# Strassen's seven products for two of three column groups of a bilinear feed-forward layer, with single buffers for turned attention weights

## The chip, the cores and the metric

The kernel runs on one core of a Trainium2 chip. The metric is the device time of one execution in microseconds (us). The kernel before takes 1522.86 us, the median of three runs (1520.39 to 1523.19).

## The reference

Thresholded attention feeds a bilinear feed-forward network, all in fp32. What is computed, cut to what matters:

```python
batch, n_heads, seq, head_dim = (8, 8, 576, 64)
scores = scale * np.matmul(q, k.transpose(0, 1, 3, 2))
thresh = np.max(scores, axis=-1, keepdims=True) - tau
scores = np.where(scores >= thresh, scores, -1000000000.0)
attn = np.exp(scores - np.max(scores, axis=-1, keepdims=True))
attn = attn / (np.sum(attn, axis=-1, keepdims=True) + 1e-09)
x = np.matmul(attn, v)            # heads put side by side: 4608 tokens x 512
a = x @ w_a                       # 512 x 1536
b = x @ w_b                       # 512 x 1536
out = a * b @ w_out               # 1536 x 512
```

The weights come as 8-byte floats and are turned to fp32 on the chip.

## The kernel before, in words

**Attention.** The work is cut into 32 pairs of heads (8 batches x 4 pairs, `HP` = 4). Each pair has five units `u`: four of 128 queries (u = 0 to 3), for both heads, and one of the 64 queries that are left over, with both heads in one. That makes 160 units `g`. The list `units` orders them by batch: first u = 0 and 1 of each of four pairs, then u = 2, 3 and 4 of each. The first batch has an order of its own. A unit runs like this:

- `scores` (L308): TensorE (PE) multiplies q and k into one PSUM tile per head (L318, a score tile `sc`). VectorE (DVE) takes the row maximum (L325), GpSimd (POOL) makes of it the exponent's bias and the threshold (L326, L327).
- `weigh` (L330): ScalarE (ACT) takes the exponent (L338), DVE zeroes what is under the threshold and sums (L342). After L342 the score tile's PSUM is free. `normalise` (L358) scales by the reciprocal.
- `turn_blocks` (L399), one unit later: DVE transposes the weights by 32 x 32 blocks into a tile `tb` (L407). u = 0 or 2 opens a new `tb`, u = 1 or 3 fills it and issues four DMAs on SyncE's (SP's) queue that write it to a scratch tensor `swap` in DRAM (L417). Unit 4 goes by a tile of its own (L422, L429).
- `turn_back` (L434), called at the head of the next unit: one DMA reads `swap` back as the turned weights `wT` (L440).
- `weighted` (L497), four units after the scores (`PV_LAG`): PE multiplies v and `wT` (L455, in `product`), ACT and DVE join the halves into a block `x` of 256 tokens (L444, L445).

The first eight units turn their weights by PE (`turn_pe`, L371).

**The feed-forward network.** 4608 tokens make 18 blocks of 256 tokens: two per batch and two of the left-over queries. `exchange_blocks` (L467) has POOL copy the two 64-row halves of a finished `x` crosswise into `xS` (L465), since all matmuls are on 64 x 64 tiles, four at a time, and each half of the rows must meet each half of the weights. `ffn` (L519) is a generator: it yields after each step of four matmuls and tells how many columns went through. The first layer has three groups of 512 hidden columns; each is two pieces `f` for two weights (`wa_sb`, `wb_sb`), and each of these is an accumulation of eight steps of 256 columns into one PSUM tile `pab` (L544). ACT copies the first into `h` (L550), DVE multiplies the second into it (L552). The second layer (L564, PSUM tile `po`) runs two accumulations of twelve steps of 512 columns, which ACT and DVE join into `osb`, and SP stores (`store`, L581). The very first block has four pieces at 128 columns, so that it can begin when half its tokens are there.

**What sets the order.** `keep_order` (L37) fixes each engine's order to that in which the program was written. In the loop over `g` (L644) every unit writes its attention work and, in four portions between them, a number of feed-forward columns by `advance` (L589): at most 0.09 of a block's, plus what replaces the weighted sums, and less when the backlog would run out before the next block is there. `make_room` (L610) places the weighted sums well inside an accumulation. PSUM is one pool, `banks` (L124), of four tiles of two banks each, which go round in turn: score tiles, `pab`, `po`, `pv` and transposes all take the next one.

**Buffers.** SBUF tiles are given out by tag: 7 for `xT` (x, xS, the left-over `xt`, raw weights), 2 each for `tb` and `wT`, 3 for loaded q and k, 4 for attention weights `w`, 6 for `h`, 5 for `osb`. A new tile of a tag waits until the readers of the one whose place it takes are done. The conversion of weights (`load_weights` to `convert_add`, L186 to L239) runs in the first 18 units, two or three pieces a unit.

Of the kernel before, what the change touches and what calls it, by code (L numbers as in the profile page):

```python
# [24 lines left out]
XT_BUFS = 7  # L25
W_BUFS = 4
WT_BUFS = 2
# [6 lines left out]
PORTIONS = (0.3, 0.35, 0.15, 0.2)  # L34

# [15 lines left out]
def kernel(  # L51
# [10 lines left out]
):  # L62

# [69 lines left out]
    def load(i, name, engine=nc.sync):  # L133

        b, hp = pairs[i]
        src = {"q": q, "k": k}[name]
        t = loads.tile([P, NB, Q], FP32, tag="qk", bufs=3, name=name + "m")
        for j in range(2):
            rows = src[b, 2 * hp + j].rearrange("(n e) d -> e n d", e=Q)
            for h in range(2):  # L140
                r = slice((2 * j + h) * Q, (2 * j + h + 1) * Q)
                engine.dma_start(t[r], rows[:, :, h * Q:(h + 1) * Q])  # L142
        loaded.setdefault(i, {})[name] = t
# [39 lines left out]
    raws, stages, extra = {}, {}, []  # L183
    state = {"loaded": 0, "converted": 0, "rows": 0}

    def load_weights(limit, engine=nc.sync):  # L186

        while (len(raws) < limit or extra) and state["loaded"] < NPIECES:
            n = state["loaded"]
            if len(raws) < limit:  # L190
                raw = work.tile([P, CW, 2], U32, tag="xT", bufs=XT_BUFS, name="raw")
            else:
                raw = extra.pop(0)
            src = pieces[n][1]
            for r, part in enumerate(src):
                dst = raw.rearrange("p f w -> p (f w)")[r * D:r * D + P // len(src)]
                if len(src) == 2:
                    dst = dst.rearrange("p (k f) -> p k f", k=2)
                engine.dma_start(dst, part)
            raws[n] = raw  # L200
            state["loaded"] = n + 1
# [46 lines left out]
    rooms = []  # L248
    for _ in range(2):
        t = work.tile([P, 2 * NB, 2 * Q], FP32, tag="tb", bufs=2, name="rows")  # L250
        t = t.rearrange("p n e -> p (n e)")[0:R]
        rooms += [t[:, c:c + 2 * NR * D].rearrange("p (n w) -> p n w", n=NR)
                  for c in range(0, 6 * NR * D, 2 * NR * D)]
    load_rows(0, "q", rooms[0])
    load_rows(0, "k", rooms[1], nc.scalar)
    load_rows(1, "q", rooms[2])
    load_rows(1, "k", rooms[3], nc.scalar)
    nc.sync.dma_start(tau_sb, tau.to_broadcast([P, 1]))
    load_weights(2)
    load_rows(2, "q", rooms[4])  # L260
    load_rows(2, "k", rooms[5])
    load_weights(4)
    load_v(0)
    for name in ("q", "k"):
        t = work.tile([P, CW, 2], FP32, tag="xT", bufs=XT_BUFS, name="rows")
        t = t.rearrange("p n e -> p (n e)")[0:R, 0:2 * NR * D]
        load_rows(3, name, t.rearrange("p (n w) -> p n w", n=NR))
# [103 lines left out]
    def turn_pe(i, u):  # L371

        ws, dg = weights.pop((i, u))
        wT = work.tile([P, NSLOT, P], FP32, tag="wT", bufs=WT_BUFS, name="wT")
# [24 lines left out]
    def turn_blocks(i, u):  # L399

        ws, _ = weights.pop((i, u))
        if u < NT:
            if u % 2 == 0:
                tbufs[i] = work.tile([P, 2 * NB, 2 * Q], FP32, tag="tb", bufs=2, name="tb")
# [11 lines left out]
            for g in range(G):  # L416
                nc.sync.dma_start(  # L417
                    swap[:, :, g * 2 * Q:(g + 1) * 2 * Q].rearrange("c p w -> p c w"),
                    tb[g * Q:(g + 1) * Q])
        else:  # L420
# [5 lines left out]
            for g in range(G):  # L426
                c = slice((1 - g // 2) * NB, (2 - g // 2) * NB)
                w0 = swap.shape[2] - TAIL + (g % 2) * Q
                nc.sync.dma_start(swap[c, :, w0:w0 + Q].rearrange("c p w -> p c w"),  # L429
                                  tb[g * Q:(g + 1) * Q])  # L430
        if part(i, u):
            ready.append(part(i, u))

    def turn_back():  # L434

        while ready:
            i, h = ready.pop(0)
            n = width(i, h)
            wT = work.tile([P, NSLOT, n], FP32, tag="wT", bufs=WT_BUFS, name="wT")
# [19 lines left out]
    def x_tile(name):  # L459
        return work.tile([P, HP, HALF], FP32, tag="xT", bufs=XT_BUFS, name=name)  # L460

# [4 lines left out]

    def exchange_blocks():  # L467
        while complete:
            x, what = complete.pop(0)
            xs = x_tile("xS")  # L470
            for hp in range(HP):
                exchange(x, xs, hp, 0, HALF, nc.gpsimd)
            blocks.append(((x, xs), what))
# [3 lines left out]
    def exchange_dma():  # L477
        while exchanges:
# [3 lines left out]
            if hp == HP - 1:  # L482
                state["rows"] = c1 // P
                if c0 == 0:
                    blocks.append(((x, xs), ("first", 0, 0)))

    def weighted_unit(i, u):
# [3 lines left out]
        if (b, 0) not in x_of:  # L491
            x_of[b, 0] = x_tile("xT")
            state["xs"] = x_tile("xS")
        join(x_of[b, 0][:, hp, u * P:(u + 1) * P], pv[:, 0], pv[:, 1])
        exchanges.append((x_of[b, 0], state["xs"], hp, u * P, (u + 1) * P))

    def weighted(i, h):  # L497
# [11 lines left out]
        if n % HALF:  # L509
            t = b % GT  # L510
            if hp == 0 and t == 0:
                xtail_of[b // GT] = x_tile("xt")
            join(xtail_of[b // GT][:, hp, t * TAIL:(t + 1) * TAIL], pv[:, 0, n - TAIL:n], pv[:, 1, n - TAIL:n])
            del loaded[i], prepared[i]
            if hp == HP - 1 and t == GT - 1:
                complete.append((xtail_of.pop(b // GT), ("tail", b - t, 0)))


    def ffn(xT, what):  # L519
# [3 lines left out]
        x, xs = xT  # L523
        hs = []
        n = CH // P
        steps = [(f, 0, HALF) for f in range(NG * n)]
        if kind == "first":
            steps = [(f, c, c + P) for c in (0, P) for f in range(2 * n)] + steps[2 * n:]
        for f, c0, c1 in steps:
            while (state["converted"] < 2 * HP * (f // n + 1)  # L530
                   or kind == "first" and state["rows"] * P < c1):
                yield 0, 0
            fs = f % n * P
            if c0 == 0:
                hs.append(work.tile([P, 2, HALF], FP32, tag="h", bufs=H_BUFS, name="h"))
            ht = hs[f][:, :, c0:c1]
            for w in (wa_sb, wb_sb):
                pab = banks(c1 - c0, "pab")
                for k in range(H):
# [7 lines left out]
                    if k < H - 1:  # L547
                        yield c1 - c0, (H - 1 - k) * (c1 - c0)
# [4 lines left out]
                yield c1 - c0, 0  # L553
        for u in range(2):
            po = banks(DM, "po")
            for F in range(NF):
                while state["converted"] < NPIECES - NF + F + 1:
                    yield 0, 0
                ht = hs[F // (2 * n) * n + F % n][:, F // n % 2]
                for r in range(2):  # L560
                    rows = slice(r * D, (r + 1) * D)
                    for c in range(2):
                        t0 = u * P + c * D
                        nc.tensor.matmul(po[c * D:(c + 1) * D, r], ht[rows, t0:t0 + D], wo_sb[rows, F, :],  # L564
                                         start=(F == 0), stop=(F == NF - 1))
                if F < NF - 1:
                    yield DM, (NF - 1 - F) * DM
# [9 lines left out]
            yield DM, 0  # L577
# [9 lines left out]
    running = {"ffn": None, "owed": 0.0, "left": 0, "done": 0, "rest": 0}  # L587

    def advance(cols):  # L589
        running["owed"] += cols  # L590
        while running["owed"] > 0:
            if running["ffn"] is None:
                if not blocks:
                    running["owed"] = 0.0
                    return
                running["ffn"] = ffn(*blocks.pop(0))
                running["left"] = BLOCK_COLS
            step, rest = next(running["ffn"], (None, 0))
# [5 lines left out]
            else:  # L604
# [3 lines left out]
                running["rest"] = rest  # L608

    def make_room():  # L610

        while running["rest"] and not (running["done"] >= ROOM and running["rest"] >= ROOM):
# [5 lines left out]
    def backlog():  # L618
        return len(blocks) * BLOCK_COLS + (running["left"] if running["ffn"] is not None else 0)
# [24 lines left out]
    for g in range(len(units) + PV_LAG):  # L644
# [6 lines left out]
        turn_back()  # L651
# [16 lines left out]
        if g == 3:  # L668
            for _ in range(2):
                t = work.tile([P, 2 * NB, 2 * Q], U32, tag="tb", bufs=2, name="raws")  # L670
                t = t.rearrange("p n e -> p (n e)")
                extra += [t[:, c:c + 2 * CW].rearrange("p (f w) -> p f w", w=2) for c in (0, 2 * CW)]
        load_weights(5 if g < 10 else 4)
        if g > BY_PE and g <= len(units):
            turn_blocks(*units[g - 1])
# [12 lines left out]
        if g > BY_PE:  # L688
            advance(PORTIONS[1] * pace)
            n = g - PV_LAG  # L690
            if BY_PE <= n < len(units) and part(*units[n]):
                make_room()
                weighted(*part(*units[n]))
                running["owed"] -= (NSLOT + 1) // 2 * width(*part(*units[n]))
        for n in early.get(g, [])[:1]:
# [12 lines left out]
        load_weights(5 if g < 10 else 4)  # L708
# [10 lines left out]
    exchange_blocks()  # L719
    while blocks or running["ffn"] is not None:  # L720
# [35 lines left out]
```

## Time and profile before

| what | value |
|---|---|
| median of three runs | 1522.86 us (1520.39 to 1523.19) |
| the profiled execution, its own time | 1518.81 us |
| its span, from the first to the last instruction | 1516.9 us |
| mean granted TensorE clock | 0.994 |
| scores L318, PE busy | 249.8 us |
| first layer L544, PE busy, all rows | 1048.8 us |
| second layer L564, PE busy | 423.2 us |
| weighted sums L455, PE busy | 190.0 us |
| HBM read and written | 127.40 and 89.65 MB |

Busy times of groups overlap, since matmuls are pipelined: the PE rows add to more than the span. PE stands for TensorE's matmuls and PEld for its weight loads. Each fp32 matmul leaves two records of each kind, so a step of four matmuls shows as eight. A row of the profile gives the line, the engine and the operation, then what it writes and reads, the shape and the count; after the first bar the busy time in us and the mean duration in ns, after the second the idle time of the engine just before and what ended it. A row of a timeline gives the start and the duration in us, and merged instructions show as a count.

### The profile page before, as it was taken

How to read it: one execution, taken by the hardware profiler on the slowest of the kernel's cores; microseconds unless marked ns; L12 is line 12 of the kernel's file. 1: busy time of each engine (PE TensorE's matmuls, PEld its weight loads, DVE VectorE, ACT ScalarE, POOL GpSimd, SP SyncE). 2: the span in 40 equal slices, each digit the busy share in tenths (PEclk: the TensorE clock that was granted, in tenths of full speed). 3: DMA queues.
4: the chain of work that ended last, by engine and by line, in shares of the span. 5: the costliest groups of instructions: out<-in, count | busy, mean ns of one | idle time of the engine just before them, and what ended most of it. 6: DMA issues, size and time to landing. Idle time of an engine off the chain costs nothing.

```text
span 1516.9 us, 51632 instructions
## 1 busy us (share of the span) xinstructions
PE 1461.7 (96%) x22896; PEld 1139.6 (75%) x22896; DVE 848.3 (56%) x1838; ACT 587.8 (39%) x929; POOL 262.3 (17%) x662
## 2 busy tenths in 40 slices
PE   6777999999999999999999999999999999999998
PEld 4666586786978587778877887777877978687775
DVE  5667676667656765675545755576646665510000
ACT  4766344444443443443333433343433443410000
POOL 2766211111110111020100101011111111110000
PEclk9999999999999999999999999999999999999999
DMA  9858888788868976796547966588748876530000
GB/s 204 177 149 217 174 164 192 179 160 192 193 148 159 192 182 150 145 195 144 123 106 146 195 145 145 124 173 176 183 90 162 184 180 132 123 75 16 2 16 15
DMA packets 625839, 220.93 MB, mean 146 GB/s; under 512 B 543184, under 2 KB 613328, under 8 KB 625616
## 3 DMA queue, kind: packets, MB, share of 16 engines
q1 hardware_dynamic: 623248, 217.04, 65.2%
q8 instruction: 180, 2.95, 0.8%
q10 hardware_dynamic: 2368, 0.59, 0.2%
q14 instruction: 43, 0.35, 0.1%
HBM read 127.40 MB, written 89.65 MB: 143 GB/s over the span
## 4 chain that ended last, share of the span: by engine, by line
PE 85%; DVE 4%; SPq 4%; DMA 3%; ACT 2%; issue 1%; POOL 0%; DVEq 0%; ACTq 0%; POOLq 0%
PE pab L544 45%; PE po L564 22%; PE sc L318 9%; PE pv L455 9%; SPq L417 2%; SPq L142 1%; DVE mx L325 1%; SPq L429 1%; DVE tb L407 1%; PE tp L380 1%; DVE low L231 0%; DVE w L342 0%; DMA swap<-tbt 0%; DMA wT<-swap 0%; DMA xS<-xT 0%
## 5 line engine op out<-in xcount | busy, mean ns | idle before, releaser
L564 PE MATMUL po<-wo_sb,h 64*64 64x512 f32 x3456 | 423.2, 589 | 0.0
L325 DVE TENSOR_REDUCE mx<-sc 128x1 f32<-128x576 f32 x288 | 205.1, 749 | 220.2 <-PE sc L318 213.8
L564 PEld LDWEIGHTS po<-wo_sb,h 64*64 64x64 f32 x3456 | 225.4, 133 | 130.5 <-issue 72.8
L338 ACT ACTIVATE w<-sc,bias,scalars 128x576 f32<-128x576 f32 x288 | 226.9, 827 | 186.7 <-POOL bias L326 181.4
L544 PE MATMUL pab<-xS,wa_sb 64*64 64x256 f32 (+1 forms) x3584 | 277.7, 370 | 4.4 <-POOL xS L465 3.3
L544 PE MATMUL pab<-xS,wb_sb 64*64 64x256 f32 (+1 forms) x3584 | 277.1, 371 | 0.5 <-issue 0.5
L361 ACT ACTIVATE w<-w,rcp 128x576 f32<-128x576 f32 x272 | 197.7, 768 | 182.0 <-DVE rcp L355 182.0
L326 POOL TENSOR_SCALAR bias<-mx,scalars 128x1 f32<-128x1 f32 x288 | 90.3, 316 | 1022.3 <-DVE mx L325 616.8
L318 PE MATMUL sc<-kT,qT 64*64 64x288 f32 x2304 | 249.8, 413 | 16.2 <-DVE kT L306 7.5
L544 PE MATMUL pab<-xT,wb_sb 64*64 64x256 f32 (+1 forms) x3200 | 248.3, 369 | 5.5 <-DVE h L552 3.9
L544 PE MATMUL pab<-xT,wa_sb 64*64 64x256 f32 (+1 forms) x3200 | 245.7, 370 | 4.1 <-POOL thr L327 2.1
L342 DVE SCALAR_TENSOR_TENSOR w<-sc,thr,w 128x576 f32<-128x576 f32 x288 | 222.4, 804 | 18.5 <-ACT w L338 15.8
L544 PEld LDWEIGHTS pab<-xS,wa_sb 64*64 64x64 f32 x3584 | 193.7, 133 | 36.8 <-POOL xS L465 10.1
L544 PEld LDWEIGHTS pab<-xS,wb_sb 64*64 64x64 f32 x3584 | 196.3, 134 | 28.2 <-issue 2.0
L544 PEld LDWEIGHTS pab<-xT,wa_sb 64*64 64x64 f32 x3200 | 174.6, 134 | 30.7 <-issue 3.3
L544 PEld LDWEIGHTS pab<-xT,wb_sb 64*64 64x64 f32 x3200 | 175.7, 133 | 27.9 <-DVE h L552 4.4
L455 PE MATMUL pv<-wT,vm 64*64 64x320 f32 (+3 forms) x2592 | 190.0, 381 | 5.6 <-ACT h L550 2.8
L318 PEld LDWEIGHTS sc<-kT,qT 64*64 64x64 f32 x2304 | 146.6, 135 | 56.6 <-issue 14.1
L407 DVE STREAM_TRANSPOSE tb<-w 128x576 f32<-128x576 f32 x240 | 171.4, 752 | 1.3 <-ACT w L361 1.3
L455 PEld LDWEIGHTS pv<-wT,vm 64*64 64x64 f32 x2592 | 146.3, 135 | 32.7 <-issue 7.7
L552 DVE TENSOR_TENSOR h<-h,pab 128x512 f32<-128x512 f32 (+1 forms) x112 | 73.1, 653 | 132.8 <-PE pab L544 128.9
L550 ACT COPY h<-pab 128x512 f32<-128x512 f32 (+1 forms) x112 | 63.5, 567 | 200.1 <-PE pab L544 199.6
(62 smaller groups left out, 702.8 us busy)
## 6 DMA issues: line engine op xcount, KB each, us to landing
swap<-tb SPq DMA_DIRECT2D x240, 288.0 KB, 5.3
wT<-swap SPq DMA_DIRECT2D x28, 1440.0 KB, 7.3
wT<-swap SPq DMA_DIRECT2D x32, 1152.0 KB, 6.2
vm<-in_v_dram SPq DMA_DIRECT2D x32, 288.0 KB, 4.8
swap<-tbt SPq DMA_DIRECT2D x128, 72.0 KB, 2.8
out_dram<-osb SPq DMA_DIRECT2D x32, 256.0 KB, 5.0
qm<-in_q_dram SPq DMA_DIRECT2D x112, 72.0 KB, 3.5
km<-in_k_dram SPq DMA_DIRECT2D x112, 72.0 KB, 4.6
```

The lines of the kernel that those rows point to most:

```text
L318: nc.tensor.matmul(sc[j if u < NT else 0][to, c], qT[r, q0:q0 + D], kT[r, c * SH:(c + 1) * SH], start=True, stop=True)
L325: nc.vector.tensor_reduce(mx[:, c], sc[j], axis=AX.XY, op=ALU.max)
L326: nc.gpsimd.tensor_scalar(bias[:, c], mx[:, c], e_nscale, None, op0=ALU.mult)
L338: nc.scalar.activation(w.rearrange("p (c k) -> p c k", c=2), s, AF.Exp, bias=bias[:, j:j + 1], scale=e_scale)
L342: nc.vector.scalar_tensor_tensor(out=wv, in0=s, scalar=thr[:, j:j + 1], in1=wv, op0=ALU.is_ge, op1=ALU.mult, accum_out=sums[:, j:j + 1])
L361: nc.scalar.activation(w, w, AF.Copy, scale=rcp[:, j:j + 1])
L407: nc.vector.transpose(tb[:, j * NB:(j + 1) * NB, (u % 2) * Q:(u % 2 + 1) * Q], w.rearrange("p (n e) -> p n e", e=Q))
L455: nc.tensor.matmul(pv[j * D:(j + 1) * D, r], vm[rows, k0], wT[rows, k0], start=(s == (NT if j == r else 0)), stop=(s == NT - 1))
L544: nc.tensor.matmul(pab[c * D:(c + 1) * D, r], w[rows, f // n, k, fs + c * D:fs + (c + 1) * D], moving, start=(k == 0), stop=(k == H - 1))
L550: nc.scalar.copy(ht, pab)
L552: nc.vector.tensor_tensor(ht, ht, pab, op=ALU.mult)
L564: nc.tensor.matmul(po[c * D:(c + 1) * D, r], ht[rows, t0:t0 + D], wo_sb[rows, F, :], start=(F == 0), stop=(F == NF - 1))
```

## The change

The first layer's products `x @ w_a` and `x @ w_b` of two of the three column groups (`STRASSEN` = 2) are done in the form of Strassen and Winograd. For such a group, tokens, inner dimension and hidden columns are each halved, which makes quarters X11 to X22 and W11 to W22. Eight products of quarters become seven of sums of quarters. One such product for both weights is eight steps of 128 columns, into a PSUM tile `seven`; it is emptied by ACT (two of seven) or by a DVE addition (five of seven) into tiles `kept` (tag `osb`); POOL makes two more sums and the four products a x b of the quarters.

- `weight_sums` makes three sums per group and weight, once, on POOL, and later replaces the quarter W12 by W11 - W12 in place. `token_sums` makes four sums per block, T1 to T4, on POOL, and their crosswise copies `tS`. Blocks whose exchange is written before the weights' sums are ready have no sums and go the old way; in the program as built this is the first block alone.
- In a block with sums, the direct group runs first, then the two groups by seven products, and the second layer takes the groups in that order.
- `exchange_blocks` takes a new block only when the block before has left its first layer.
- Room: `wT` and `tb` have one buffer instead of two, loaded q and k two instead of three. x tiles have three, xS, t and tS share three, `xt` has one. Raw weights and the first rows of q and k lie in the room of the sums until these are made.
- `turn_back` issues at most one read-back: only when no turned weights are waiting, and not in the unit that wrote the swap; it is called at the head of a unit and again after `weighted`.
- `advance`, `make_room` and `backlog` count a block's columns by its kind; room is at most half of an accumulation.

The diff, cut to its core:

```diff
-XT_BUFS = 7
-WT_BUFS = 2
+X_BUFS = 3
+STRASSEN = 2
...
-        t = loads.tile([P, NB, Q], FP32, tag="qk", bufs=3, name=name + "m")
+        t = loads.tile([P, NB, Q], FP32, tag="qk", bufs=2, name=name + "m")
...
+    NSUM = STRASSEN * 2 * 3 * HP * P
+    sums_u32 = const.tile([P, NSUM], U32, name="sums_u32")
...
-                tbufs[i] = work.tile([P, 2 * NB, 2 * Q], FP32, tag="tb", bufs=2, name="tb")
+                tbufs[i] = work.tile([P, 2 * NB, 2 * Q], FP32, tag="tb", bufs=1, name="tb")
...
-    def turn_back():
-
-        while ready:
-            i, h = ready.pop(0)
+            ready.append((part(i, u), g))
+
+    def turn_back(g):
+
+        if ready and not turned and ready[0][1] < g:
+            (i, h), _ = ready.pop(0)
             n = width(i, h)
-            wT = work.tile([P, NSLOT, n], FP32, tag="wT", bufs=WT_BUFS, name="wT")
+            wT = work.tile([P, NSLOT, n], FP32, tag="wT", bufs=1, name="wT")
...
+    def quarter(w, f, k, c):
+
+        return w[:, f].rearrange("p (s k e) f -> p s k e f", s=2, k=2)[:, :, k, :, c * P:(c + 1) * P]
+
+    def weight_sums(f, y, w, last):
+        q = [[quarter(w, f, k, c) for c in range(2)] for k in range(2)]
...
+        tt = nc.gpsimd.tensor_tensor
+        if not last:
+            tt(s1, q[0][1], q[1][1], op=ALU.add)
+            tt(s2, s1, q[0][0], op=ALU.subtract)
+            tt(s4, q[1][0], s2, op=ALU.subtract)
+        else:
+            tt(q[0][1], q[0][0], q[0][1], op=ALU.subtract)
+
     def exchange_blocks():
-        while complete:
+        while complete and not state["xs"]:
...
+    def token_sums():
...
+            tt(t1, x12, x11, op=ALU.subtract)
+            tt(t2, x22, t1, op=ALU.subtract)
+            tt(t3, x22, x12, op=ALU.subtract)
+            tt(t4, x21, t2, op=ALU.subtract)
+            for hp in range(HP):
+                exchange(t, ts, hp, 0, HALF, nc.gpsimd)
...
+            seven = [(W11, X11), (S2, T2), (W21, X21), (S1, T1), (S3, T3), (S4, X22), (W22, T4)]
...
+            for m, (wq, xq) in enumerate(seven):
+                acc = banks(2 * P, "seven").rearrange("p r (w q) -> p r w q", w=2)
+                for y in range(2):
+                    for s in range(2):
+                        for e in range(2):
+                            for r in range(2):
+                                rows = slice(r * D, (r + 1) * D)
+                                for c in range(2):
+                                    nc.tensor.matmul(
+                                        acc[c * D:(c + 1) * D, r, y], wq[y][rows, s, e, c * D:(c + 1) * D],
+                                        xq[s][rows, e], start=(s + e == 0), stop=(s + e == 2))
...
+                if m == 0:
+                    k1 = keep()
+                    nc.scalar.copy(k1, acc)
+                elif m == 1:
+                    k6 = keep()
+                    dve(k6, k1, acc, op=ALU.add)
+                elif m == 2:
+                    dve(k1, k1, acc, op=ALU.add)
+                    times(h1[:, :, 0:P], k1)
+                elif m == 3:
+                    k5 = keep()
+                    nc.scalar.copy(k5, acc)
+                elif m == 4:
+                    k7 = keep()
+                    dve(k7, k6, acc, op=ALU.add)
+                    pool(k6, k6, k5, op=ALU.add)
+                    pool(k5, k5, k7, op=ALU.add)
+                    times(h2[:, :, P:HALF], k5)
+                elif m == 5:
+                    dve(k6, k6, acc, op=ALU.add)
+                    times(h1[:, :, P:HALF], k6)
+                else:
+                    dve(k7, k7, acc, op=ALU.add)
+                    times(h2[:, :, 0:P], k7)
...
-        turn_back()
+        turn_back(g)
+        token_sums()
         exchange_blocks()
...
                 weighted(*part(*units[n]))
                 running["owed"] -= (NSLOT + 1) // 2 * width(*part(*units[n]))
+                turn_back(g)
```

Here `times` is a POOL multiplication of a kept tile's halves, `keep` takes a tile of tag `osb`, and `dve` and `pool` are the tensor_tensor operations of these engines.

## The prediction

> **What bounds the kernel now.** I read the engines' busy time and the slices of the span first, then a table by stage.
>
> ```profile
> span 1516.9 us, 51632 instructions
> PE 1461.7 (96%) x22896; PEld 1139.6 (75%) x22896; DVE 848.3 (56%) x1838; ACT 587.8 (39%) x929; POOL 262.3 (17%) x662
> ...
> PE   6777999999999999999999999999999999999998
> ```
>
> ```profile
> 60.00:200.00 140.00, 116.20 (x2248) 87.47 (x2246) 94.67 (x205) 80.30 (x143) 75.33 (x104) 0.97 0.72 174
> 200.00:650.00 450.00, 444.30 (x6961) 347.36 (x6957) 298.83 (x654) 195.86 (x295) 63.10 (x208) 1.00 0.79 171
> 650.00:1360.00 710.00, 709.50 (x11044) 562.15 (x11040) 404.26 (x874) 265.98 (x405) 95.88 (x306) 1.00 0.68 148
> ```
>
> The columns are PE, PEld, DVE, ACT, POOL, clock, DMA share, GB/s. From 200 us on PE has no gap: 1153.8 of 1160 us. So a column of matmul saved there is time saved, and a wait added to PE is time lost. DVE is 66% busy from 200 to 650 us, 57% after. The next view, PE in order of time, gives the price of a step (four 64x64 tiles, eight records) at 128 and at 256 columns:
>
> ```profile
> 79.15 1.05 PE L544 MATMUL pab<-xT,wb_sb 64*64 64x128 f32 x32
> 80.02 1.05 PE L544 MATMUL pab<-xS,wb_sb 64*64 64x128 f32 x32
> ```
>
> ```profile
> 547.03 1.83 PE L544 MATMUL pab<-xS,wb_sb 64*64 64x256 f32 x28
> ...
> 548.76 1.83 PE L544 MATMUL pab<-xT,wa_sb 64*64 64x256 f32 x28
> ```
>
> Start to start, four steps take 0.87 us at 128 columns (0.2175 each) and 1.73 at 256 (0.4325). Half the columns cost half the time, although the weight loads per column double. This decides whether seven products in place of eight can pay at all. The remaining prices are rows by shape:
>
> ```profile
> L325 DVE TENSOR_REDUCE mx<-sc 128x1 f32<-128x576 f32 x288 | 205.1, 749 | 220.2 <-PE sc L318 213.8
> L342 DVE SCALAR_TENSOR_TENSOR w<-sc,thr,w 128x576 f32<-128x576 f32 x288 | 222.4, 804 | 18.5 <-ACT w L338 15.8
> L407 DVE STREAM_TRANSPOSE tb<-w 128x576 f32<-128x576 f32 x240 | 171.4, 752 | 1.3 <-ACT w L361 1.3
> L552 DVE TENSOR_TENSOR h<-h,pab 128x512 f32<-128x512 f32 x104 | 69.9, 672 | 127.3 <-PE pab L544 126.8
> L465 POOL COPY xS<-xT 64x256 f32<-64x256 f32 x120 | 47.6, 396 | 37.2 <-DVE xT L445 30.2
> L242 POOL TENSOR_TENSOR wb_sb<-wb_sb,low 128x512 int32<-128x512 int32 x12 | 15.2, 1279 | 9.2 <-DVE wb_sb L237 9.2
> ```
>
> DVE instructions overlap by some 0.07 us, so in a row they cost 0.70, 0.74, 0.69 and 0.61.
>
> [...] the int32 row above has 1.28, which I use, and half for 256. [...]
>
> **The change, part by part.**
>
> *Matmuls.* 17 of 18 blocks, all but the first, take the new path for two column groups: 34 groups. One group was 32 steps of 256: 32 x 0.4325 = 13.84 us. It becomes 7 x 8 = 56 steps of 128: 12.18 us at 0.2175, 12.49 at 0.223 (median over all 128-column stretches of the first block, run-in included). Saved per group 1.66 to 1.35; over 34 groups 46 to 56 us. I take 52.
>
> *PSUM.* A group was emptied four times, two on ACT and two on DVE; now seven times, two on ACT and five on DVE: 102 more DVE adds, 102 x 0.61 = 62 us of DVE work, all in the Strassen stretches (14,336 of a block's 34,816 columns). The four PSUM buffers go round in turn, so each allocation waits for the fourth before it. A product lasts 1.74 us where a direct result lasted 3.46, so PE comes round twice as fast. In the program order of the changed kernel one unit reads: scores end at 0; product A ends at 0.22 us, B runs to 1.95, C next, in A's buffer. DVE has two reductions (1.40) and two transposes (1.37) ahead of A's add (0.61), so A is free at 3.4 and C starts 1.4 us late. Most units are kinder, with C in slack. Adding rows in this way along the 61 units that hold Strassen products gives 5 to 15 us; I take 12.
>
> *One tb instead of two.* This is the new wait. The transposes of a unit that opens a new tb now wait until the four swap DMAs of the unit just before have read the old one. It occurs at 31 places in the program (u = 0, 1 of a pair, then the next pair's). Before shows the chain it waits for, on DVE and then on SP's queue:
>
> ```profile
> 547.07 1.43 DVE L407 STREAM_TRANSPOSE tb<-w 128x576 f32<-128x576 f32 x2
> ...
> 554.90 1.43 DVE L407 STREAM_TRANSPOSE tb<-w 128x576 f32<-128x576 f32 x2
> ```
>
> ```profile
> 548.53 4.40 SPq L417 DMA_DIRECT2D swap<-tb  x4
> 557.63 0.38 SPq L440 DMA_DIRECT2D wT<-swap  x1
> ```
>
> The first pair of transposes closes the old tb at 548.50; the swap is issued at once, and the read-back L440, which waits for it, starts at 557.63: 9.1 us. The next transposes stood ready at 554.90, so with one buffer they wait 2.7 us. Measured so at all 31 places of before, the excess is 130 us, 4.2 on average (0.2 to 10.2), as SP's loads sometimes go ahead of the swap. In the changed kernel a wait also gives SP time, so delays don't pile up; from the 9.1 us and unit lengths of 6.8 (early) to 8.1 us (late) I get 3.7 to 2.4. I take 3.2, about 100 us of DVE wait. Behind it on DVE queue the adds that free PSUM and L342, which frees the scores' two buffers. What PE loses: 13 places lie in Strassen stretches with some 0.5 us of slack, 13 x 2.7 = 35 us; 18 lie beside direct or second-layer products of 3.5 to 10 us, where 0.8 us each is left, 15 us. Together 50. From below: 15, if DVE's idle time takes most of it; from above, every wait as in before and in full where it meets Strassen, 100.
>
> *POOL.* Per block 4 quarter sums and 8 copies (4 x 0.65 + 8 x 0.40 = 5.8 us), per group 4 quarter products and 2 sums (4 x 0.65 + 2 x 1.28 = 5.2 us): 17 x 5.8 + 34 x 5.2 = 275 us, and some 18 us once for the weights' sums. POOL goes from 262 to about 555 us and stays under 40%. The token sums lie beside the previous block's second layer (12,288 columns, 20 us) and the direct group (13.8 us); were that cover gone, 17 x 9 us would show. But the softmax's bias (L326) can queue behind a 3.2 us chain of sums: 0 to 10 us, I take 3.
>
> *Moves at no cost.* The single wT: its read-back is issued after the preceding pv instead of at a unit's start; it lands in 7.3 us and is needed two units (14 us) later. SP waits there for PE; loads and stores behind it are needed units later. Three x tiles instead of seven shared: each is free over 60 us before it is written again. Raw weights and first rows lie in the sums' room: as many in flight as before. Cover gone, each would cost a few us once.
>
> **Sum.** -52 + 12 + 50 + 3 = +13 us on the profiled 1518.8: 1532. The three runs' median lies 4 us above that execution, so I predict 1536 us.
>
> **Rivals.**
> 1. *The DVE wait is absorbed* (ends faster). DVE idles 2.7 us ahead of its reductions in the shown unit and is 57% busy after 650 us; if it makes up there what it waited, PE loses only 15 us: -52 + 15 + 8 = -29, 1494 us. The decision point is the loss per place: below (52 - 15) / 31 = 1.2 us the change is a gain. Against it: the wait stands ahead of L342, not in DVE's idle time at the unit's end.
> 2. *SP's backlog stays.* Each swap as late as in before: wait 100, slots 15, bias 8, gain 46: +77, 1600 us. For it: swap issues up to 5 us late in before; against: waiting gives SP time.
> 3. *The products don't run at 0.2175.* If loads bind at the stage's rate (562.15 / 11040 = 51 ns) 8 loads make a 0.41 us step, 34 x 56 x 0.19 = +360 us. The 128-column stretch with the same loads excludes this nearly: 2%.
>
> **How the numbers follow.** Forecast with its slower neighbours (1526 to 1576) 50%, rival 2 and beyond 8%, rival 3 2%, rival 1 and what lies below no change 32%, within 0.2% (3 us, about what a measurement can tell from no change) 8%. Slower 0.60, same 0.08, faster 0.32. The range runs from 1490 (gain 56, wait 15, slots 5, from the median: 1487, cut a little) to 1578, leaving 10% at each end. The likeliest case's own range is 1526 to 1576.
>
> **What would show it.** Right: DVE transposes tb waiting for DMA swap, about 30 times and 3 us; PE gaps ended by DVE kept, DVE w or ACT; PE's busy time near 1410. Products at 1.74 us apart in the last 150 us, where no attention runs. Wrong: no DVE wait over 1 us on the swap, or PE gaps as small as before (then 1494); steps well over 0.22 us; PE waiting for POOL.

## The result and the profile after

The changed kernel takes 1645.45 us (median of four runs, 1642.18 to 1647.92), the kernel before beside it 1522.51 us (1520.39 to 1523.19): a ratio of 1.0809, 95% interval 1.0787 to 1.0831. The direction was the predicted one; the size was not: 1536 was predicted, with a range of 1490 to 1578, and the time lies 67 us above it.

The page of the changed kernel: span, busy times, and the slices of PE and of the TensorE clock that was granted.

```profile
span 1646.0 us, 65397 instructions
...
PE 1476.8 (90%) x29424; PEld 1186.3 (72%) x29424; DVE 918.1 (56%) x1940; ACT 586.3 (36%) x929; POOL 565.9 (34%) x1086
...
PE   6777888898899988999999989998899989999998
...
PEclk9998988999899999999999999998999999999999
```

Before, PE stood at 9 in every slice from the fifth to the last but one. Now eights lie all along the span, and eights in the clock's row too. PE's busy time went up by 15 us where the prediction awaited some 1410. Busy time alone would hide this: the same columns at a lower clock are busy for longer (of the products' steps, those wholly at half clock have a median of 0.427 us, all together 0.218).

By stage (the columns are PE, PEld, DVE, ACT, POOL, clock, DMA share, GB/s):

```profile
200.00:650.00 450.00, 396.66 (x7957) 316.21 (x7953) 280.25 (x597) 169.34 (x257) 141.90 (x305) 0.95 0.70 152
650.00:1360.00 710.00, 657.42 (x13240) 535.25 (x13236) 423.40 (x893) 253.59 (x385) 229.79 (x487) 0.98 0.65 141
```

PE now stands still for 53 us of the first stretch and for 53 us of the second, where it had stood still for 6 us in both together, and the clock of the first stretch fell from 1.00 to 0.95. The waits of PE and of DVE, each with us in total, times, and the longest:

```profile
PE seven L661 <- issue: 27.7, 29, 2.6
PE sc L332 <- DVE kT L305: 16.4, 6, 5.5
PE seven L661 <- DVE kept L671: 14.4, 5, 5.7
PE seven L661 <- DVE kept L680: 10.7, 4, 4.5
```

```profile
DVE mx L339 <- PE sc L332: 189.5, 97, 9.3
...
DVE tb L423 <- DMA swap<-tb: 89.1, 24, 7.1
```

The DVE wait is the announced one, nearly to the number: 24 waits, 89 us, 3.7 us each. The first row of PE was in no step of the prediction: "issue" says that PE waited for nothing that the profile shows. Rows two to four end with DVE, as announced, but with up to 5.7 us each.

One of the 24 waits in order of time shows how it reaches PE. DVE, then PE, then SP's queue, then the busy times by stretch (columns as above), all of the changed kernel:

```profile
592.74 1.41 DVE L339 TENSOR_REDUCE mx<-sc 128x1 f32<-128x576 f32 x2
600.12 1.44 DVE L423 STREAM_TRANSPOSE tb<-w 128x576 f32<-128x576 f32 x2 [5.97 <-DMA swap<-tb]
601.48 0.78 DVE L356 SCALAR_TENSOR_TENSOR w<-sc,thr,w 128x576 f32<-128x576 f32 x1
...
602.92 0.77 DVE L305 STREAM_TRANSPOSE kT<-km 128x576 f32<-128x576 f32 x1
```

```profile
595.19 1.94 PE L617 MATMUL pab<-xT,wb_sb 64*64 64x256 f32 x32
596.91 2.37 PE L471 MATMUL pv<-wT,vm 64*64 64x256 f32 x36
603.75 1.86 PE L332 MATMUL sc<-kT,qT 64*64 64x288 f32 x16 [4.47 <-DVE kT L305]
```

```profile
587.49 2.11 SPq L159 DMA_DIRECT2D vm<-in_v_dram  x1
589.64 0.68 SPq L724 DMA_DIRECT2D out_dram<-osb  x1
590.42 5.18 SPq L433 DMA_DIRECT2D swap<-tb  x4
```

```profile
600.00:602.00 2.00, 0.00 (x0) 0.00 (x0) 1.88 (x3) 0.00 (x0) 1.15 (x3) 1.00 0.39 40
602.00:604.00 2.00, 0.25 (x4) 0.21 (x8) 2.00 (x7) 0.00 (x0) 0.00 (x0) 1.00 0.91 316
604.00:606.00 2.00, 2.00 (x24) 1.16 (x20) 0.60 (x3) 1.44 (x2) 0.00 (x0) 0.54 1.08 315
606.00:608.00 2.00, 2.00 (x32) 1.24 (x28) 2.00 (x4) 1.08 (x2) 0.84 (x3) 0.61 0.74 198
```

The swap's four DMAs go out from 590.42 behind a load and a store, and free the tile at 600.12. DVE stands at its transposes for 5.97 us. Queued behind them are L356 and, last, L305: the turn of the *next* pair's k. PE finishes what it has, at 599.3, and then stands before the scores that need this k for 4.47 us. When it starts again, its clock is at 0.54 and 0.61 for the next 4 us. So one DVE wait of 6.0 us costs PE 4.5 us of standing and some 1.7 us of slow running (half of the 3.41 us that the clock's record gives for this window), even though the work at hand was a direct group, where the prediction counted 0.8 us.

### The profile page after: what moved, and what is told of

The parts are those of the page before. It is cut to its first block, busy times and chain, and to the rows that moved or that the text cites. A ratio compares the mean times of both kernels' runs of the same rounds, so it can differ in the third digit from the quotient of the medians.

```text
span 1646.0 us, 65397 instructions
## 1 busy us (share of the span) xinstructions
PE 1476.8 (90%) x29424; PEld 1186.3 (72%) x29424; DVE 918.1 (56%) x1940; ACT 586.3 (36%) x929; POOL 565.9 (34%) x1086
## 5 line engine op out<-in xcount | busy, mean ns | idle before, releaser
L356 DVE SCALAR_TENSOR_TENSOR w<-sc,thr,w 128x576 f32<-128x576 f32 x288 | 222.6, 805 | 20.7 <-ACT w L352 17.3
L423 DVE STREAM_TRANSPOSE tb<-w 128x576 f32<-128x576 f32 x240 | 171.7, 753 | 102.4 <-DMA swap<-tb 89.1
L651 POOL TENSOR_TENSOR h<-kept 128x256 f32<-128x256 f32 x136 | 97.2, 728 | 237.2 <-DVE kept L673 176.4
L661 PE MATMUL seven<-t,sums_u 64*64 64x128 f32 x2176 | 119.8, 280 | 25.6 <-DVE kept L671 14.4
L460 ACT COPY xT<-pv 128x256 f32<-128x256 f32 (+1 forms) x68 | 24.4, 359 | 278.1 <-PE pv L471 278.1
L661 PEld LDWEIGHTS seven<-t,sums_u 64*64 64x64 f32 x2176 | 95.3, 138 | 31.4 <-DVE kept L671 16.0
L661 PE MATMUL seven<-tS,sums_u 64*64 64x128 f32 x2176 | 116.1, 280 | 0.7 <-issue 0.6
L617 PE MATMUL pab<-xS,wa_sb 64*64 64x256 f32 (+1 forms) x1408 | 100.6, 366 | 9.8 <-DMA xS<-xT 5.9
L461 DVE TENSOR_TENSOR xT<-xT,pv 128x256 f32<-128x256 f32 (+1 forms) x68 | 27.4, 403 | 132.8 <-ACT xT L460 132.7
L617 PE MATMUL pab<-xT,wb_sb 64*64 64x256 f32 (+1 forms) x1280 | 92.7, 363 | 5.4 <-DVE h L625 2.5
L617 PE MATMUL pab<-xS,wb_sb 64*64 64x256 f32 (+1 forms) x1408 | 96.1, 365 | 0.0
L661 PEld LDWEIGHTS seven<-tS,sums_u 64*64 64x64 f32 x2176 | 93.3, 139 | 1.7 <-issue 1.4
```

Source lines behind the costliest of these rows:

```text
L356: nc.vector.scalar_tensor_tensor(out=wv, in0=s, scalar=thr[:, j:j + 1], in1=wv, op0=ALU.is_ge, op1=ALU.mult, accum_out=sums[:, j:j + 1])
L423: nc.vector.transpose(tb[:, j * NB:(j + 1) * NB, (u % 2) * Q:(u % 2 + 1) * Q], w.rearrange("p (n e) -> p n e", e=Q))
L617: nc.tensor.matmul(pab[c * D:(c + 1) * D, r], w[rows, f // n, k, fs + c * D:fs + (c + 1) * D], moving, start=(k == 0), stop=(k == H - 1))
L651: pool(out, t[:, :, 0], t[:, :, 1], op=ALU.mult)
L661: nc.tensor.matmul(acc[c * D:(c + 1) * D, r, y], wq[y][rows, s, e, c * D:(c + 1) * D], xq[s][rows, e], start=(s + e == 0), stop=(s + e == 2))
```

## The experiments

Ten kernels, each timed beside the kernel before on the same chip (1518.5 to 1521.2 us). "Half clock" below is the time that the clock's record of the profiled execution gives at 0.5, mostly in windows of 3.4 or 6.8 us; some 2 us of it lie outside the span in every row. It costs about half of itself, as a step of the products takes twice as long there (0.427 against 0.218 us in the changed kernel).

| kernel | us | ratio [95% interval] | PE's gaps, us | half clock, us |
|---|---|---|---|---|
| before | 1522.5 | 1 | 44.8 | 21.5 |
| before, one tb | 1593.27 | 1.0465 [1.0437, 1.0492] | 93.3 | 73.3 |
| changed, no sums | 1607.83 | 1.0563 [1.0532, 1.0594] | 103.5 | 85.8 |
| changed, no sums, two tb | 1525.17 | 1.0036 [1.0025, 1.0048] | 48.5 | 34.7 |
| changed, two tb | 1556.09 | 1.0238 [1.0201, 1.0274] | 95.2 | 48.0 |
| changed | 1645.45 | 1.0809 [1.0787, 1.0831] | 158.6 | 115.6 |
| changed, late transposes | 1573.67 | 1.0354 [1.0306, 1.0403] | 111.8 | 40.8 |
| changed, products in pairs | 1744.33 | 1.1467 [1.1438, 1.1496] | 241 | 138.6 |
| changed, two tb, 64x128 products | 1539.12 | 1.0131 [1.0091, 1.0172] | 65.5 | 28.1 |
| changed, late transposes, 64x128 products | 1556.28 | 1.0238 [1.0198, 1.0278] | 71.2 | 41.9 |
| before at 128 columns | 1649.16 | 1.0852 [1.0799, 1.0904] | 117.7 | 43.1 |
| before at 128 columns, 64x128 | 1624.51 | 1.0679 [1.0648, 1.0711] | 54.4 | 42.8 |

The gaps are summed over all matmul records of a trace, counting every pause over 50 ns.

**One tb in the kernel before.** Only the number of buffers is changed; the raw rows of the start get a tile of their own for their second place.

```diff
-                tbufs[i] = work.tile([P, 2 * NB, 2 * Q], FP32, tag="tb", bufs=2, name="tb")
+                tbufs[i] = work.tile([P, 2 * NB, 2 * Q], FP32, tag="tb", bufs=1, name="tb")
```

> The kernel before with one change alone: tb has one buffer (its second one, needed for rows and raw weights at the start, becomes a tile of its own). No Strassen. Theory A (the DVE wait for the swap costs PE, and the gaps cost again by half-clock windows): some 30 waits of DVE on the swap, 80 to 120 us in sum, PE idle up by 30 to 45 us, half-clock time up by some 40 us, 1570 to 1600 us. Rival B (the loss comes from emptying seven products through four PSUM buffers): 1525 to 1540, since direct results leave slack. Rival C (single wT and the other moved steps): 1522 to 1530.

Measured: 1593.27 us, 72 us more. DVE and PE:

```profile
DVE tb L407 <- DMA swap<-tb: 81.5, 24, 8.8
```

```profile
PE sc L318 <- DVE kT L291: 26.6, 6, 7.6
PE pv L455 <- issue: 11.8, 4, 4.3
```

Of the span's 76.9 us, 48.5 are added gaps and 25.9 are half of the added half clock: 74.4. There is no product in this kernel, so the wait costs this much without one: 2.0 us of gaps for each of the 24 waits. Again the turned k (here L291) is what PE stands before.

**The change without its sums.** All blocks go the direct way; the single buffers, the rooms and the order of read-backs stay.

```diff
-        if not converting and not state["sums"]:
+        if not converting and not state["sums"] and STRASSEN > 2:
```

> The changed kernel with all its buffers and moved steps, but the sums are never made, so every block goes the direct way: the buffering without Strassen. Theory A: as the run with one tb in the kernel before, within 10 us, 1570 to 1605. Rival B: 1525 to 1545. Rival C: over 20 us slower than the run with one tb alone.

Measured: 1607.83 us, 15 us above the kernel before with one tb: more than theory A allowed and less than rival C asked for.

**The change with two tb.** To make room, the second layer's weights hold six of their twelve chunks.

```diff
-                tbufs[i] = work.tile([P, 2 * NB, 2 * Q], FP32, tag="tb", bufs=1, name="tb")
+                tbufs[i] = work.tile([P, 2 * NB, 2 * Q], FP32, tag="tb", bufs=2, name="tb")
...
-                        nc.tensor.matmul(po[c * D:(c + 1) * D, r], ht[rows, t0:t0 + D], wo_sb[rows, F, :],
+                        nc.tensor.matmul(po[c * D:(c + 1) * D, r], ht[rows, t0:t0 + D], wo_sb[rows, F % (NF // 2), :],
```

> The changed kernel with two tb buffers. To make room, w_out keeps six of its twelve chunks of rows (chunk F is read at place F modulo 6), so the second layer computes with half of the weights, by the same matmuls. Theory A: the wait for the swap is gone, PE idle down by some 65 us and half-clock time down by some 40 us, 1540 to 1575. Rival B: 1625 to 1645. Rival C: 1630 to 1645.

Measured: 1556.09 us, 89 us under the changed kernel. No DVE wait on the swap is left. But it is still 35 us slower than before: without the wait the change still loses. PE's first row and the stretches:

```profile
PE seven L661 <- issue: 28.9, 30, 3.2
```

```profile
200.00:650.00 450.00, 429.31 (x8801) 351.86 (x8797) 306.50 (x659) 187.19 (x286) 150.05 (x332) 1.00 0.76 165
650.00:1360.00 710.00, 677.47 (x14027) 563.09 (x14023) 444.00 (x935) 265.94 (x403) 241.79 (x512) 1.00 0.68 148
1360.00:1545.00 185.00, 184.00 (x4116) 162.96 (x4108) 38.66 (x67) 21.00 (x38) 51.98 (x81) 1.00 0.14 36
```

The clock is back at 1.00. PE still stands for 53 us of the 1160, and "issue" is the largest part of it. In the last stretch, which holds products too, it stands for 1 us: there the DMA share is 0.14 in place of 0.68 to 0.76.

**No sums and two tb.** Both edits together.

> The changed kernel with two tb tiles and with no sums made, so that all blocks take the direct way; as with the other two-tb kernel, the second layer uses half of its weights for the same matmuls to make room. What is left of the change is one wT, two loaded q and k, the x tiles' tags, the raw weights' rooms and the order of the read-backs. Theory that these cost nothing by themselves, and that the 15 us they cost beside one tb came from that wait: 1520, at most 1525 us. Theory that they cost by themselves: 1530 to 1536. In the first case all of the 38 us that the changed kernel loses with two tb tiles lies with the products.

Measured: 1525.17 us, 4.9 us over the 1520.25 of before beside it (the ratio's interval: 0.25 to 0.48%). So the other single buffers and rooms cost 5 us, not 15, when the swap isn't waited for; the remaining 10 us came only beside the one tb. One PE wait is new against before, and 6.8 us of half clock follow it:

```profile
PE pab L617 <- DMA xS<-xT: 5.9, 1, 5.9
```

**Late transposes.** The changed kernel with one tb, but the transposes that open a tb (u = 0, 2) are written after `weigh`, behind L356, and so no longer stand ahead of it.

```diff
-        if g > BY_PE and g <= len(units):
+        opens = g <= len(units) and units[g - 1][1] in (0, 2)
+        if g > BY_PE and g <= len(units) and not opens:
...
+        if g > BY_PE and opens:
+            turn_blocks(*units[g - 1], g)
```

> The changed kernel with one tb, all computed; only the transposes that open a new tb (u = 0, 2) are written after the unit's L356 (the thresholding, L342 before) instead of ahead of it, so the swap they wait for has some 3 us more and the score buffers don't queue behind them. Theory A (wait on the swap, then half-clock windows): DVE's waits on the swap fall from 89 to under 20 us and the time comes near that with two tb buffers, 1550 to 1575. Rival (the later swap makes the weighted sums wait for wT, and the gain is given back): PE pv waits for DMA wT rise over 20 us, 1610 or more.

Measured: 1573.67 us, 72 us under the changed kernel, with the DVE wait on the swap down from 89.1 to 25.3 us (under 20 was expected) and half clock down from 115.6 to 40.8 us. The place of a wait in a queue is worth nearly as much as the second buffer (89). "Issue" stays:

```profile
DVE tb L423 <- DMA swap<-tb: 25.3, 18, 4.4
```

```profile
PE seven L661 <- issue: 31.6, 31, 3.1
```

**Products in pairs.** Two successive products share one PSUM tile, so that there are more products' rooms per buffer.

```diff
-                acc = banks(2 * P, "seven").rearrange("p r (w q) -> p r w q", w=2)
+                if m % 2 == 0:
+                    two = banks(4 * P, "seven")
+                acc = two[:, :, m % 2 * 2 * P:(m % 2 + 1) * 2 * P].rearrange("p r (w q) -> p r w q", w=2)
```

> The changed kernel, but two successive products of seven share one PSUM tile (each used half of its columns), so PE comes round to a buffer every 3.5 us as with direct results. Theory A: only the gaps at products outside the waits go, some 40 us of idle time and 15 us of clock, 1590 to 1610. Rival B: most of the loss goes, 1500 to 1540. Rival C: 1630 to 1645.

Measured: 1744.33 us, slower by 99, where all three expectations had a gain or no change. The waits of PE tell why it is no test of PSUM:

```profile
PE seven L663 <- DVE kept L682: 59.8, 31, 6.0
PE seven L663 <- DVE kept L675: 54.0, 28, 5.4
PE seven L663 <- ACT kept L670: 24.4, 26, 2.5
```

The three lines are the emptyings of the first product of each tile: the second waits until the first has been emptied, which fits a tile whose two halves are followed as one. The edit brought a wait of its own; it shows only how dear a wait of a product on its emptying is.

**Products on 64x128 tiles, two tb.** As the two-tb kernel, with one matmul for each pair that shares its tokens: the same columns in half the instructions.

```diff
-                                for c in range(2):
-                                    nc.tensor.matmul(
-                                        acc[c * D:(c + 1) * D, r, y], wq[y][rows, s, e, c * D:(c + 1) * D],
-                                        xq[s][rows, e], start=(s + e == 0), stop=(s + e == 2))
+                                nc.tensor.matmul(acc[:, r, y], wq[y][rows, s, e], xq[s][rows, e],
+                                                 start=(s + e == 0), stop=(s + e == 2))
```

> The run with two tb (w_out kept as six of twelve chunks, so the second layer uses half of its weights) with the seven products on 64x128 tiles instead of 64x64: half as many PE instructions in the products, the same columns. Theory D (PE runs out of fetched instructions, 28.9 us in 30 gaps named issue): these gaps fall under 6 us and the time to 1515 to 1535. Rival E (the gaps are something of the products themselves, such as the sums' addresses): gaps and time stay, 1550 to 1560. If a weight load of 128 columns is not hidden, a step goes over 0.25 us and the time over 1580.

Measured: 1539.12 us, 17 us less and 4 us above what theory D had. "Issue" is gone from the products' waits; the largest row that is left there is one of emptying:

```profile
PE seven L660 <- DVE kept L678: 3.3, 3, 1.2
```

The table of DMA queues has one of instructions, q8 (packets, MB, share): before, the change with two tb, and this kernel.

```profile
q8 instruction: 180, 2.95, 0.8%
```

```profile
q8 instruction: 231, 3.78, 1.0%
```

```profile
q8 instruction: 171, 2.80, 0.8%
```

A packet is 16 KB (2.95 MB in 180). The change adds 6528 matmul and 6528 load records of PE, and 231 - 180 = 51 packets: 13056 / 51 = 256 records to a packet. By matmul records, gaps included, the products take 38 us less than with 64x64 tiles (496.3 to 458.6), but the scores 17 us more (169.5 to 186.6), though their matmuls are the same.

**Late transposes and 64x128 products** with one tb, nothing left out.

> All computed: the changed kernel with the opening transposes written after L356 and the products on 64x128 tiles. If theories A and D hold, what is left of the loss is gaps at products for PSUM (some 13 us) and a little clock, against 46 to 56 us of saved columns: 1505 to 1540. If the late transposes give back, over 1580.

Measured: 1556.28 us. Both savings stand side by side: 89 us under the changed kernel. It is still 38 us slower than before, and 16 us above the expected range.

**The kernel before at 128 columns.** All first-layer steps are halved: neither single buffers nor sums, nor a product.

```diff
+        else:
+            steps = [(f, c, c + P) for f in range(NG * n) for c in (0, P)]
```

> The kernel before, without Strassen and with two tb, but every first-layer step at 128 columns instead of 256: the same columns, twice the instructions and twice the emptyings of half the size. Theory D: gaps named issue of 30 to 60 us appear in pab, 1565 to 1600. Rival E: no such gaps; twice the fixed cost per step and some gaps for PSUM alone, 1530 to 1545.

Measured: 1649.16 us, 131 us more for the same columns. Theory D had the waits for issue right, but its time is 49 us too low.

```profile
PE pab L546 <- issue: 52.6, 61, 2.8
PE pab L546 <- DVE w L342: 10.5, 16, 1.6
PE pab L546 <- DVE h L554: 8.8, 11, 2.5
```

Over a whole kernel "half the columns cost half the time", the price on which the prediction rested, does not hold. By matmul records, gaps included, the first layer's 1664 steps of 256 and 128 steps of 128 became 3456 steps of 128, and PE's time for them went from 789.6 to 922.1 us: 0.267 us a step, where 0.2175 was taken. Of these 132 us more, 72 are gaps (86.7 against 14.5 us, most of it issue) and 60 lie within the work. Before has hardly a wait for issue at its first layer:

```profile
PE pab L544 <- issue: 1.4, 2, 0.9
```

**The same on 64x128 tiles.**

```diff
-                        for c in range(2):
-                            nc.tensor.matmul(pab[c * D:(c + 1) * D, r],
-                                             w[rows, f // n, k, fs + c * D:fs + (c + 1) * D], moving,
-                                             start=(k == 0), stop=(k == H - 1))
+                        nc.tensor.matmul(pab[:, r], w[rows, f // n, k, fs:fs + P], moving,
+                                         start=(k == 0), stop=(k == H - 1))
```

> The kernel before with all first-layer steps at 128 columns, as in the run that took 1649 us, but each pair of 64x64 matmuls that share their tokens is one matmul on a 64x128 tile: the same columns in half as many instructions, about as many as in the kernel before, and the same smaller PSUM tiles and emptyings. Theory that PE runs out of fetched instructions at 128-column steps: the gaps ended by issue (52.6 us in 61) fall under 5 us, and the time falls to 1545 to 1590, what is left being a step of 0.223 us in place of 0.2175, switches between kinds of matmul, and the emptyings. Rival, that the emptying of twice as many PSUM tiles on DVE and ACT makes the loss: it stays above 1620.

Measured: 1624.51 us: neither theory holds as it stood. No row of issue is left among PE's largest waits (down to 2.3 us), and the first layer's gaps fall from 86.7 to 27.5 us. The rival's emptyings are small too:

```profile
PE pab L545 <- DVE w L342: 7.3, 12, 1.5
PE pab L545 <- DVE h L552: 6.8, 7, 2.4
```

But the time falls by 25 us only, and the first layer still takes 855.3 us, 66 more than at 256 columns. Against the run before it the first layer, gaps included, takes 67 us less and the scores take 35 us more (166 to 201 us), though their matmuls are the same; the second layer takes 10 us more. So with the wide tile the 52.6 us of waits for issue are gone, and a cost appears at the matmuls of the other form, as in the kernel with two tb. That it arises where tiles of both forms meet is a reading; no run separates it.

## Why the prediction was wrong, step by step

The first split is by kernels that differ in one group of edits (the moves, the sums, the tb; the halved second-layer weights come in with the first and go with the last): from before to "no sums, two tb" +5 us, from there to "changed, two tb" +31, from there to "changed" +89, together 125 of the measured 123. The prediction had 0, -37 (-52 + 12 + 3) and +50 for the same three. The second split is by what PE worked on. It adds, over all matmul records, the time from a record's start to the start of the next, with the gap ahead of a kind of matmul counted with that kind (the 1048.8 us of busy time given for the first layer of before leave out the rows of the left-over queries, which are counted here):

```
us of PE, gaps included   before   no sums, two tb   changed, two tb   changed
pab (direct)               789.6       795.1             313.6          318.2
seven (products)               -           -             496.3          527.4
sc (scores)                162.1       163.1             169.5          196.1
po (second layer)          362.7       362.5             366.7          373.5
pv (weighted sums)         155.6       157.6             157.9          184.7
```

*Matmuls, -52: failed.* The step that failed reads "Half the columns cost half the time" and took it for 1904 steps from a stretch of four. The 34 groups took 795.1 - 313.6 = 481.5 us as direct ones and 496.3 as products, so 15 us more where 52 less were predicted: 67 us of error, with the wait on the swap out of play. 1904 steps at 0.2175 would be 414 us, and most steps run at that (median 0.218 in every stage). The 82 us over it are 41.5 us of gaps (28.9 for issue, 12.6 for PSUM and the rest) and 40.7 us within the work. (That this makes 67 us of error and not 82 is because the direct groups, too, took 11 us more than 34 x 13.84, and because 52 was taken where the price alone gave 56.) Of the 40.7, some 13 come with the gaps: a record after which PE waits lasts its full 0.27 us before the gap begins to count, 54 times 0.24 more than in a row. The rest lies around changes to another kind of matmul (7 to 13, by how many neighbours are counted), in hesitations of 0.14 to 0.2 us that leave no gap (5 to 10), and in half clock (some 4); what causes the first two is open. The four steps were not misread: the 1746 steps that have no pause and no other matmul in them average 0.225 us. What failed is to take them for all. Split steps in the kernel before take 0.267 us each, the products in the changed kernel with two tb 0.261 (496.3 / 1904): the halved step costs this with no sums near it. Nor are the waits for issue all of it: on 64x128 tiles, where no row of them stands among the largest, a step still averages 0.241 in the products (458.6 / 1904) and 0.247 in the first layer (855.3 / 3456).

*What the issue waits are.* By the counts above a packet of queue q8 goes with 256 of PE's records. A step is 16 records (eight matmuls, eight loads), so a packet lasts 16 steps, 3.5 us at 128 columns and 6.9 at 256. In the kernel with two tb each of the 27 gaps for issue over 0.3 us comes 1.2 to 1.9 us after the end of such a packet. Where the DMA engines are 0.68 to 0.76 busy the gaps for issue of the products are 28 us in 1160; in the last 185 us, with a packet every 4.0 us (median) but the share at 0.14, they are 0.9 us. That instructions arrive late behind other DMAs fits all of this. Halving the instructions took the rows of issue (28.9 and 52.6 us) out of the waits in both pairs of kernels, though the form of the tile changed with it. No run took the other DMAs away while it kept the instructions, and attention, too, is nearly over in the last stage; so the part that the DMAs play is a reading of stages, not an experiment. The name alone proves nothing: the waits for issue at the weighted sums (8.1 us in 3 in the changed kernel, 11.8 in 4 in before with one tb) come 3.7 to 11.2 us after such a packet and are under 1 us with two tb. What they wait for is not shown.

*PSUM, +12: right.* PE's gaps at products other than issue are 12.6 us in the kernel with two tb. In the changed kernel L671 and L680 rise to 14.4 and 10.7 us, but those are the swap's delay, handed on by DVE: with two tb they are 2.4 and 3.8.

*One tb, +50: the DVE side was right, the conversion failed.* 24 waits and 89 us stand against 31 and 100. Two things were off in "What PE loses". First, the slack of 3.5 to 10 us beside direct or second-layer products, where "0.8 us each" was to be left, isn't there: without any product the 24 waits cost 2.0 us of gaps each. PE's order is fixed too, and it comes to scores whose k hangs behind the waiting transposes on DVE's queue (L305). The prediction named the adds and L342 as what is queued there, not the turn of k. PE's gaps rise by 158.6 - 95.2 = 63 us between the kernels with one and two tb, 0.7 us for each us of DVE's wait: 16 at scores that wait for that k, 19 at products that wait for L671 and L680 (the adds that the prediction did name), the rest in smaller rows. Second, the clock was in no step. Its record of the changed kernel has the values 1 and 0.5 alone, and half clock in 15 windows of 3.41 us, nine of 6.83 and one of 2.94 at the end. Of the 24 gaps of 2 us or more in the changed kernel 20 meet such a window, of the 27 of 1 to 2 us only 3; with late transposes it is 5 of 11. Half clock rises by 67.6 us, of which half, 34 us, is lost. 63 + 34 = 97, against 96.2 us between the two spans. So each us of DVE's wait cost 1.1 us of the kernel. In the kernel before with one tb it was 48.5 + 25.9 for 81.5.

*POOL, +3: right.* PE's waits for POOL's copies xS are 3.9 us (3.3 before), the other 0.9. POOL is busy 566 us, 555 were predicted; the quarter products took 0.73 us, 0.65 were taken. One wait was in no term: DVE's add L685 waits 24.8 us for POOL's sum L681, but PE waits for L685 only 3 us with two tb and 7 in the changed kernel.

*Moves at no cost: nearly.* 5 us, one wait of 5.9 us for a block's exchange among them; and 10 us more beside one tb. The SP queue stands longer before its read-backs there (L456 <- PE pv: 162 us in the changed kernel, 80 with two tb), which fits, but it was not tried alone.

*The rivals.* 1, an absorbed wait, is excluded by the kernel before with one tb: +72 us. 2, "SP's backlog stays", came closest with 1600 us, by luck: it has PE lose 100 us to the wait, and the second tb gave back 89, but by swaps as late as in before (130 us of DVE wait by the prediction's count, where 89 were measured) and not by the turned k and the clock; and it kept a gain of 46 us from the products. 3, steps at 0.41, is excluded by the median of 0.218; but its question, whether the products run at 0.2175, was the right one, and the 2% were spent on one mechanism only.

*The sign announced for it* could not have warned: "products at 1.74 us apart in the last 150 us, where no attention runs" came true (1.75 from 1500 us on, median). That stage has next to no DMA load (a share of 0.04 from 1500 to 1640 us) and no attention.

No kernel here beats the one before; the closest with products, 1539.12 us, keeps two tb at the expense of half of the second layer's weights. What is open: what the products' steps lose apart from the waits for issue, the cost of mixed forms of tile, and the 10 us beside one tb.

## What to carry to other kernels

When a change trades columns for instructions, price it over a stretch of many packets of instructions with the work and the DMA load of the place where it will run, not over four steps; here the halved step took 0.26 us where four of them had shown 0.2175. When a buffer is taken away, list everything behind the waiting instruction on its queue up to the next thing that the bottleneck engine needs, and price a stop of PE with what follows it: here a us of DVE's wait cost 1.1 us, a third of it through the clock. And a wait can be moved: writing the waiting transposes one step later in the queue gave back 72 of 89 us without a byte of room.

## What was not expected of the hardware

- PE stands in waits that fit the late arrival of its own instructions: 27.7 us in 29 waits in the changed kernel, 52.6 in 61 when before's steps are halved, 1.4 in 2 at the first layer of before, whose steps are nearly all of 256 columns, and no row of over 2.4 us at these matmuls on 64x128 tiles.
- A single gap of 2 us or more on PE can bring 3.4 or 6.8 us at half clock (20 of 24 such gaps in the changed kernel, 10 of 14 in before with one tb, 5 of 11 with late transposes).
- Scores on 64x64 tiles take 35 us more (166 to 201) when the first layer's steps around them are on 64x128 tiles, and 17 more (169.5 to 186.6) when the products are.
